# Hedgehog attention and a squared-ReLU feed-forward on one core: q loads, x buffers, the last chunk's stores, the holds of loads and the written order

## The chip, the cores and the metric

The kernel runs on one core of one Trainium2 chip. The metric is the device time of one execution in microseconds (us); lower is better. Three runs of the kernel before gave 361.65, 359.49 and 361.79 us, with a median of 361.65 us.

## What is computed

There are two stages. The first is linear attention with a feature map over q and k (8 batches, 8 heads, 576 tokens, head size 64). The second is a feed-forward over the 4608 tokens.

```python
def phi(x):
    proj = np.einsum('bhsd,df->bhsf', x, w_phi)                  # 64 -> 128
    proj = proj - np.max(np.abs(proj), axis=-1, keepdims=True)
    return np.concatenate([np.exp(proj), np.exp(-proj)], axis=-1)
q_p, k_p = (phi(q), phi(k))
kv = np.einsum('bhsf,bhsd->bhfd', k_p, v)
z = np.sum(k_p, axis=2)
num = np.einsum('bhsf,bhfd->bhsd', q_p, kv)
den = np.einsum('bhsf,bhf->bhs', q_p, z)[..., None] + 1e-06
x = (num / den), heads side by side: 4608 tokens x 512
h = np.maximum(x @ w_in, 0.0)                                    # 512 -> 2048
out = h * h @ w_out                                              # 2048 -> 512, float32
```

## The kernel before, in words

**Tiles and stages.** `attention(b)` (L295) makes x of one batch. Of the 576 tokens of a batch, 512 form a chunk of four tiles of 128 tokens; the last 64 tokens of all eight batches together form a ninth chunk. So the feed-forward has nine chunks, 0 to 8, of 512 tokens. For each chunk `ffn_in` (L710) does 16 groups of four matmuls of 128x512 (L692), a ReLU out of PSUM (L669 on ScalarE or L671 on VectorE) and a square on VectorE (L678). `ffn_out` (L751) does for each of the four token tiles 16 such matmuls in four parts (L757), a copy out of PSUM into one of three `ot` buffers (L192 or L190), and a store by SyncE's queue (L772, L775). Chunk 0 goes through `ffn_in_small` (L703), in 16 groups of sixteen 128x128 matmuls. Within attention, k and q are transposed (batches 0 and 1 by TensorE, L307; batches 2 to 7 by DMA, L317), projected with `w_phi` (L333), reduced to a maximum (L388, L489), put through two exponentials (L394, L539), and so on to `xo` (L578), which is transposed into `xT` or `xS` by a DMA of SyncE's queue (L612).

**What sets the order.** The Python builds a list of steps in program order (`Plan.add`, L61) and then issues them in the order of a list of 1755 numbers, `ORDER` (L831), which is written out by hand for all engines. Each engine takes its steps strictly in that order (`pin`, L135). `BASES` (L919) gives each step's PSUM bank, `STATES` (L926) chooses between ScalarE and VectorE for the 231 steps that may go to either, and `GATES` (L931) holds a load on the GpSimd queue until a named step has ended. `FILL` (L946) puts groups of idle matmuls (L825, 128 columns each, 120 in all) ahead of 13 TensorE steps in the first 30 us, to keep TensorE running.

**Loads.** All loads of k, q, v and weights are issued by GpSimd, with a cast from float32 to bfloat16. k and v of batches 2 to 7 come in four pieces of two heads (`load`, L240), four tokens in a row to a partition. q comes in eight (`load_q`, L259): four head pairs times two halves of two tokens each. Tile t of the q buffer (128 columns) then holds head t mod 8, tokens 2(t div 8) and the next; `q_ts` (L469) names the four tiles of a step, which lie side by side.

**Stores.** A token tile of chunks 0 to 7 is stored in one DMA of 128 rows of 2 KB (L775). A tile of the last chunk holds 64 tokens of two batches; tiles 0 to 2 are stored in two DMAs of 64 rows each (L772), on SyncE's queue. The last tile goes through `last_out` (L709) in halves of 256 columns, and each half is stored in two DMAs of 64 rows (L744), one issued by SyncE and one by ScalarE.

**Rings.** There are three `ot` buffers, three `xo` buffers (L174) and two `xT`. An `ot` copy has to wait until the store that last read its buffer has landed.

Of the kernel before, what the change touches and what calls it, by code (L numbers as in the profile page):

```python
# [15 lines left out]
SEM = 0.045  # L16
# [8 lines left out]
def dve_cost(n):  # L25
    return n / 960 + 0.064, n / 960 + 0.150 + SEM

# [80 lines left out]
def kernel(  # L108
# [52 lines left out]
    warm = sb("warm", [P])  # L161
# [9 lines left out]
    NXT = 2  # L171
    assert B * S == NCH * TCH and NCH == B + 1 and S == TCH + 64
    qp, qn = ring("qp", NQP, [8 * P]), ring("qn", NQP, [8 * P])
    xo = ring("xo", 3, [8 * D])  # L174
    rden = ring("rden", 3, [8], F32)
# [11 lines left out]
    def copy(out, in_):  # L187

        if now[0].eng == "DVE":
            pin(nc.vector.tensor_copy(out=out, in_=in_))  # L190
        else:
            pin(nc.scalar.activation(out=out, in_=in_, func=ACT.Copy))  # L192

# [65 lines left out]
    def load_q(b, jjs=(0, 1), single=True, release=False, prs=((0, 4),)):  # L259

        x = xq[b % 2]
        for jj in jjs:
# [10 lines left out]
    def of(tag, b, us):  # L273
        qs = [("xq", b % 2, u, a) for u in us if u != "s" for a in range(3)] if tag == "xq" else []
        return qs + [(tag, b % 2, u) for u in us if u != "s"] + [(tag, b % 2, "s", hi) for u in us if u == "s" for hi in range(2)]
# [19 lines left out]
    def attention(b):  # L295
# [122 lines left out]
        def scaled(t, x, n):  # L418

            e = t[:, :, D:].to_broadcast([t.shape[0], n, 2, D // 2]).rearrange("p m c x -> p m x c")  # L420
            pin(nc.vector.tensor_tensor(out=t[:, :, :D].rearrange("p m (x c) -> p m x c", c=2),  # L421
                                        in0=x.rearrange("p (m x c) -> p m x c", m=n, c=2), in1=e, op=ALU.mult))

        def v_ops(g0, g1):

            gs = [4] if g0 == 4 else list(range(g0, g1))
            for sg in range(2):
# [9 lines left out]
                def fn(t=t):  # L437
                    scaled(t[:, 8 * g0 : 8 * g1, :], xv[s2][:, 512 * g0 : 512 * g1], 8 * (g1 - g0))
                add("DVE", dve_cost(256 * (g1 - g0)), fn, r=of("xv", b, gs) + [("ve", s2, sg, g) for g in gs],
                    w=[("va", s2, sg, g) for g in gs], what="V")  # L440
# [28 lines left out]
        def q_ts(c):  # L469
            if c == 4:  # L470
                return [16, 17]
            return [8 * (c // 2) + h for h in range(8)] if first else [8 * (c // 2) + 4 * (c % 2) + i for i in range(4)]
# [36 lines left out]
        def q_ops(c):  # L509
# [3 lines left out]
            def fn():  # L513
                o = ps2(pf)
                for u in range(2):
# [5 lines left out]
                    else:  # L521
                        r = slice(64 * u, 64 * u + 64)
                        rhs = qTb[r, ts[0] : ts[-1] + 1, :]
# [19 lines left out]
        def out_ops(c):  # L543
# [27 lines left out]
            xs = xslot[0] % 3  # L571
# [92 lines left out]
    def relu_sq(g, dst, toks):  # L664
# [9 lines left out]
        def fn():  # L674
# [3 lines left out]
            pin(nc.vector.tensor_tensor(out=dst, in0=i_, in1=i_, op=ALU.mult))  # L678
        add("DVE", dve_cost(256), fn, r=[("hr", sl)], w=toks, what="sq")
# [6 lines left out]
    def ffn_in(c, mc):  # L686
# [8 lines left out]
        relu_sq(g, h2[c % 2][mc // 4][:, mc % 4, :], [("h2", c % 2, mc, tt) for tt in range(4)])  # L695

    def ffn_in_small(c, tt, mg):
# [10 lines left out]
        relu_sq(g, h2[c % 2][mg][:, :, tt * P : (tt + 1) * P], [("h2", c % 2, mg * 4 + i, tt) for i in range(4)])  # L708
# [4 lines left out]
    def last_out(c, tt, part):  # L713
# [26 lines left out]
        for half in range(2):  # L740
            for u, (name, e) in enumerate((("SP", nc.sync), ("ACT", nc.scalar))):
                def fn(half=half, u=u, e=e):
                    b = 2 * tt + u
                    pin(e.dma_start(out=out[b * S + 512 : b * S + 576, half * 256 : half * 256 + 256],  # L744
                                    in_=otl[u * 64 : u * 64 + 64, half * 256 : half * 256 + 256]))
                add(name, (0.5, 2.4), fn, r=[("otl", half)], what="stl")

    def ffn_out(c, tt, part):
# [12 lines left out]
        if part == 3:  # L761
# [6 lines left out]
            for u in range(2 if c == NCH - 1 else 1):  # L768
                def fn(u=u):
                    if c == NCH - 1:  # L770
                        b = 2 * tt + u
                        pin(nc.sync.dma_start(out=out[b * S + 512 : b * S + 576, :], in_=ot[sl][u * 64 : u * 64 + 64, :]))  # L772
                    else:
                        o = out[c * S : c * S + 512, :].rearrange("(p j) n -> j p n", j=4)[tt]
                        pin(nc.sync.dma_start(out=o, in_=ot[sl]))  # L775
                add("SP", (0.5, 0), fn, r=[("ot", sl)], dma=(0.37 if c == NCH - 1 else 0.74, HW_IN, "st"), what="st")
# [43 lines left out]
    for op in plan.arrange():  # L820
        if op.seq in FILL:
            now[0] = filler
            bank, n = FILL[op.seq]
            for _ in range(n):
                pin(nc.tensor.matmul(out=psum[:, bank, :P], lhsT=warm, rhs=warm, start=True, stop=True))  # L825
# [6 lines left out]
    4, 5, 1, 0, 9, 13, 15, 2, 3, 6, 12, 8, 14, 40, 10, 41, 11, 7, 42, 19, 43, 44, 64, 18, 46, 65, 16, 66, 45, 47,  # L832
    67, 21, 109, 68, 111, 110, 17, 70, 112, 69, 48, 144, 71, 20, 72, 119, 145, 141, 26, 120, 122, 73, 29, 146, 142,
    75, 123, 51, 22, 86, 52, 23, 50, 87, 53, 124, 76, 115, 54, 88, 116, 55, 77, 90, 89, 113, 79, 78, 56, 114, 91,
    59, 80, 27, 94, 92, 35, 83, 155, 61, 63, 95, 74, 98, 49, 34, 169, 85, 62, 104, 57, 93, 100, 25, 103, 60, 58,
    101, 158, 102, 84, 81, 99, 97, 127, 143, 105, 82, 106, 96, 159, 107, 125, 24, 128, 108, 129, 126, 156, 160, 131,
    382, 130, 170, 219, 132, 213, 157, 121, 133, 214, 147, 134, 220, 172, 148, 135, 173, 28, 117, 136, 149, 137,
    118, 174, 150, 161, 151, 199, 231, 200, 162, 183, 197, 37, 232, 184, 138, 163, 198, 33, 215, 139, 164, 187, 140,
    152, 165, 188, 380, 322, 216, 189, 36, 166, 323, 325, 153, 185, 217, 167, 154, 385, 221, 168, 233, 222, 337,
    326, 218, 331, 234, 223, 374, 334, 327, 332, 338, 224, 328, 379, 324, 225, 335, 38, 329, 175, 340, 235, 339,  # L840
    330, 376, 343, 171, 333, 236, 176, 352, 336, 341, 344, 342, 177, 190, 226, 353, 346, 178, 179, 186, 246, 381,
    261, 191, 347, 286, 180, 262, 287, 192, 355, 378, 193, 288, 194, 207, 349, 383, 208, 181, 209, 182, 264, 345,
    195, 210, 356, 502, 375, 196, 211, 265, 377, 506, 239, 350, 370, 263, 227, 245, 248, 212, 277, 367, 238, 228,
    30, 237, 240, 278, 358, 242, 229, 247, 371, 364, 244, 357, 384, 254, 253, 230, 241, 243, 510, 256, 372, 368,
    255, 39, 249, 369, 257, 373, 348, 250, 279, 251, 359, 32, 361, 351, 266, 31, 258, 354, 259, 252, 365, 280, 362,
    201, 281, 203, 260, 520, 393, 204, 202, 282, 267, 283, 295, 284, 524, 296, 268, 289, 514, 297, 290, 285, 270,
    360, 304, 271, 291, 305, 528, 392, 515, 292, 532, 366, 293, 269, 272, 306, 298, 363, 307, 299, 556, 533, 308,
    294, 205, 300, 206, 585, 560, 301, 302, 390, 309, 313, 303, 273, 310, 576, 564, 314, 274, 311, 275, 316, 276,
    315, 538, 317, 312, 575, 441, 472, 574, 442, 568, 516, 473, 577, 318, 444, 578, 319, 474, 542, 445, 571, 546,
    391, 320, 394, 573, 569, 438, 321, 395, 402, 443, 550, 589, 403, 396, 592, 503, 397, 439, 404, 582, 507, 389,  # L850
    551, 405, 499, 572, 508, 398, 446, 417, 504, 500, 454, 387, 525, 455, 509, 386, 399, 511, 526, 779, 456, 527,
    521, 388, 512, 400, 776, 410, 505, 463, 522, 517, 775, 401, 523, 580, 539, 501, 464, 593, 518, 581, 543, 440,
# [126 lines left out]
```

## Time and profile before

| what | value |
|---|---|
| runs (us) | 361.65, 359.49, 361.79; median 361.65 |
| profiled execution: span from first to last instruction | 358.8 us |
| what lies around the span, against the median | 2.85 us |
| TensorE busy | 341.0 us (95%), 3411 matmuls |
| VectorE busy | 276.7 us (77%) |
| ScalarE busy | 227.1 us (63%) |
| GpSimd busy | 112.8 us (31%), nearly all of it issuing loads |
| granted TensorE clock | 0.997 |
| DMA packets | 102631, 39.62 MB; under 512 B 77248 |
| GpSimd's queue (q0) | 51744 packets, 18.36 MB, 48.4% of 16 DMA engines |

The profile's own time is given only as a span, so the difference of 2.85 us to the median covers both what lies around a span and the difference between runs. A matmul's end is modelled in the profile: a row of four 128x512 matmuls reads 1.03 us long but the next row starts 0.87 us after it, so starts are the better measure of what a step costs TensorE. "PE" is TensorE's matmul side, "DVE" VectorE, "ACT" ScalarE, "POOL" GpSimd, "SP" SyncE; a "q" behind the name is its sequencer, which issues DMAs.

### The profile page before, as it was taken

To read this page: it belongs to the slowest core of one execution; us is meant where nothing else is said; L and a number is where in the kernel's file an instruction comes from. 1 tells how busy PE (TensorE), PEld (TensorE's weight loads), DVE (VectorE), ACT (ScalarE), POOL (GpSimd) and SP (SyncE) were. 2 spreads that over 40 slices of the span, in tenths; PEclk is the share of its full clock that TensorE was granted. 3 is DMA by queue.
4 is the path that set the end of the run, shared out by engine and by line. 5 is a ranking of instruction groups with operands and counts; after the bars stand their busy time and mean duration, and the time that the engine had idled before them with its cause. 6 is when DMAs were issued, how large, how long until landed. Compare 5 with 4: busy or idle time off the path is not lost.

```text
span 358.8 us, 8512 instructions
## 1 busy us (share of the span) xinstructions
PE 341.0 (95%) x3411; PEld 193.6 (54%) x3444; DVE 276.7 (77%) x525; ACT 227.1 (63%) x428; POOL 112.8 (31%) x167
## 2 busy tenths in 40 slices
PE   5989999979999999999999999999999998999994
PEld 4779975524554555455544644455555543444442
DVE  3999998869979997989778878799988816736210
ACT  3999887379779775796678577769777210340301
POOL 8845550784707930299301820000000000000000
PEclk9999999999999999999999999999999999999998
DMA  9999989999979998799956995600401121010105
GB/s 103 177 200 201 175 95 157 161 143 192 117 161 123 159 120 179 175 96 140 127 111 116 97 192 97 151 9 29 62 31 51 50 82 38 3 60 0 58 25 153
DMA packets 102631, 39.62 MB, mean 110 GB/s; under 512 B 77248, under 2 KB 98112, under 8 KB 102592
## 3 DMA queue, kind: packets, MB, share of 16 engines
q0 software_dynamic: 51744, 18.36, 48.4%
q1 hardware_dynamic: 50608, 20.55, 26.4%
q8 instruction: 27, 0.44, 0.5%
q10 hardware_dynamic: 240, 0.16, 0.2%
q14 instruction: 12, 0.10, 0.1%
HBM read 36.77 MB, written 9.44 MB: 129 GB/s over the span
## 4 chain that ended last, share of the span: by engine, by line
PE 72%; DVE 11%; ACT 9%; DMA 5%; issue 2%; SPq 0%; DVEq 0%; ACTq 0%; POOLq 0%
PE psum L757 27%; PE psum L692 24%; PE psum L554 5%; PE psum L333 4%; PE psum L703 3%; PE psum L449 3%; DVE va L421 3%; DMA out_dram<-ot 3%; PE psum L524 2%; ACT kp L394 2%; ACT kn L394 2%; DVE mq L489 2%; DVE h L678 2%; ACT hr L669 1%; DVE mk L367 1%
## 5 line engine op out<-in xcount | busy, mean ns | idle before, releaser
L757 PE MATMUL psum<-wout,h 128*128 128x512 bf16 x527 | 128.3, 380 | 2.5 <-issue 1.3
L692 PE MATMUL psum<-xT,win 128*128 128x512 bf16 x448 | 106.3, 379 | 3.9 <-ACT ot L192 2.5
L669 ACT ACTIVATE hr<-psum 128x512 bf16<-128x512 f32 x96 | 55.3, 596 | 48.2 <-PE psum L692 25.8
L757 PEld LDWEIGHTS <-h 128*128 128x128 bf16 x560 | 50.2, 98 | 54.3 <-issue 1.1
L692 PEld LDWEIGHTS <-win 128*128 128x128 bf16 x512 | 47.4, 97 | 58.0 <-issue 8.0
L678 DVE TENSOR_TENSOR h<-hr 128x512 bf16<-128x512 bf16 x144 | 56.4, 416 | 16.8 <-ACT hr L669 16.0
L539 ACT ACTIVATE qp<-psum 128x1024 bf16<-128x1024 f32 (+1 forms) x40 | 37.4, 940 | 23.1 <-PE psum L524 22.7
L265 POOL DMA_DIRECT2D xq<-in_q_dram x52 | 38.8, 764 | 33.8 <-ACT en L496 21.2
L489 DVE TENSOR_REDUCE mq<-psum 128x8 f32<-128x1024 f32 (+1 forms) x40 | 44.1, 1111 | 3.6 <-PE psum L333 2.9
L388 DVE TENSOR_REDUCE mk<-psum 128x8 f32<-128x1024 f32 (+1 forms) x35 | 38.2, 1111 | 3.1 <-PE psum L333 3.1
L671 DVE TENSOR_SCALAR hr<-psum 128x512 bf16<-128x512 f32 x48 | 32.8, 687 | 9.4 <-PE psum L692 7.9
L394 ACT ACTIVATE kp<-psum 128x1024 bf16<-128x1024 f32 (+1 forms) x35 | 32.8, 937 | 9.6 <-DVE mk L388 8.0
L539 ACT ACTIVATE qn<-psum 128x1024 bf16<-128x1024 f32 (+1 forms) x40 | 37.5, 940 | 1.5 <-PE psum L554 1.2
L394 ACT ACTIVATE kn<-psum 128x1024 bf16<-128x1024 f32 (+1 forms) x35 | 32.8, 937 | 0.0
L421 DVE TENSOR_TENSOR va<-xv,va 64x256 bf16<-64x256 bf16 (+2 forms) x68 | 30.4, 462 | 1.6 <-ACT va L413 0.8
L192 ACT ACTIVATE ot<-psum 128x512 f32<-128x512 f32 x18 | 10.7, 593 | 31.8 <-PE psum L757 27.3
L566 DVE TENSOR_TENSOR psum<-psum,en 128x520 f32<-128x520 f32 (+1 forms) x40 | 27.6, 698 | 3.8 <-PE psum L554 2.5
L578 DVE TENSOR_TENSOR xo<-psum,rden 128x512 bf16<-128x512 f32 (+1 forms) x40 | 27.4, 686 | 0.8
L245 POOL DMA_DIRECT2D xv<-in_v_dram x26 | 19.5, 757 | 23.3 <-DMA out_dram<-ot 20.8
L190 DVE COPY ot<-psum 128x512 f32<-128x512 f32 x17 | 11.6, 684 | 16.1 <-PE psum L757 9.4
L245 POOL DMA_DIRECT2D xk<-in_k_dram x28 | 21.1, 760 | 5.5 <-ACT va L407 3.5
L449 PE MATMUL psum<-va,kp 128*128 128x65 bf16 x256 | 19.6, 193 | 0.9 <-DVE va L421 0.4
(67 smaller groups left out, 402.4 us busy)
## 6 DMA issues: line engine op xcount, KB each, us to landing
out_dram<-ot SPq DMA_DIRECT2D x32, 256.0 KB, 2.8
xk<-in_k_dram POOLq DMA_DIRECT2D x26, 128.0 KB, 3.9
xq<-in_q_dram POOLq DMA_DIRECT2D x48, 64.0 KB, 3.9
xv<-in_v_dram POOLq DMA_DIRECT2D x24, 128.0 KB, 3.6
win<-in_moe_w_in_dram POOLq DMA_DIRECT2D x4, 512.0 KB, 11.7
wout<-in_moe_w_out_dram POOLq DMA_DIRECT2D x4, 512.0 KB, 9.4
xq<-in_q_dram POOLq DMA_DIRECT2D x4, 256.0 KB, 5.0
xv<-in_v_dram POOLq DMA_DIRECT2D x2, 512.0 KB, 9.1
```

Source lines behind the costliest of these rows:

```text
L245: pin(nc.gpsimd.dma_start(out=x[:, a * 512 : z * 512].rearrange("p (h x) -> p h x", x=4 * D), in_=src[b][2 * a : 2 * z, 0:512, :].rearrang ...
L265: pin(nc.gpsimd.dma_start(out=x[:, jj * 1024 + a * 256 : jj * 1024 + z * 256].rearrange("p (h x) -> p h x", x=128), in_=q[b][2 * a : 2 * z ...
L388: pin(nc.vector.tensor_reduce(out=mk_view(g), in_=ps2(pj)[:, :, : n * Fd].rearrange("p e (i f) -> p e i f", f=Fd), axis=AX.X, op=ALU.max, ...
L394: pin(nc.scalar.activation(out=dst[slot][:, :, :n, :].rearrange("p e i f -> p e (i f)"), in_=ps2(pj)[:, :, : n * Fd], func=ACT.Exp, scale= ...
L421: pin(nc.vector.tensor_tensor(out=t[:, :, :D].rearrange("p m (x c) -> p m x c", c=2), in0=x.rearrange("p (m x c) -> p m x c", m=n, c=2), i ...
L489: pin(nc.vector.tensor_reduce(out=mqb[:, c, :, :n], in_=ps2(pj)[:, :, : n * Fd].rearrange("p e (i f) -> p e i f", f=Fd), axis=AX.X, op=ALU ...
L539: pin(nc.scalar.activation(out=o, in_=i_, func=ACT.Exp, scale=sgn))
L669: pin(nc.scalar.activation(out=hr[sl], in_=ps1(g), func=ACT.Relu))
L671: pin(nc.vector.tensor_scalar(out=hr[sl], in0=ps1(g), scalar1=0.0, scalar2=None, op0=ALU.max))
L678: pin(nc.vector.tensor_tensor(out=dst, in0=i_, in1=i_, op=ALU.mult))
L692: pin(nc.tensor.matmul(out=o, lhsT=win[mc // 4][:, kc, mc % 4 * P : (mc % 4 + 1) * P], rhs=x, start=(kc == 0), stop=(kc == KC - 1)))
L757: pin(nc.tensor.matmul(out=ps1(g), lhsT=h2[c % 2][mc // 4][:, mc % 4, tt * P : (tt + 1) * P], rhs=wout[mc // 4][:, mc % 4, :], start=(mc = ...
```

## The change

1. **q of batches 2 to 7** is loaded by four tokens of a head pair, as k and v are: four DMAs of 128 KB to a batch in place of eight of 64 KB. The tiles of a step then lie two apart, so the moving operand of the projection (L524) steps over every second tile.
2. **Five `xo` and `rden` buffers** in place of three.
3. **The last chunk's tiles** are stored whole: one DMA of 128 rows for tiles 0 to 2, and one DMA of 128 rows for each half of the last tile. The pattern on the output side is two blocks of 64 rows, 576 rows apart.
4. **GATES** names 108 loads in place of 131, other steps for each; **ORDER**, **BASES** and **STATES** are new. By the flags, three ReLUs, five `ot` copies and three transposed copies move from VectorE to ScalarE and two `kv` copies the other way.
5. **FILL** has 90 matmuls of 248 columns ahead of 14 steps, and writes them in part into columns from 264 on of a bank in use; `warm` is 256 columns wide.
6. `pool_cost`, `engine()` and `plan.either((o, "POOL", ...))` could move work to GpSimd, but `LENT = 0` turns all of it off.

```diff
-    xo = ring("xo", 3, [8 * D])
-    rden = ring("rden", 3, [8], F32)
+    xo = ring("xo", 5, [8 * D])
+    rden = ring("rden", 5, [8], F32)
...
         x = xq[b % 2]
+        if b >= 2:
+            for a, z in prs:
+                def fn(a=a, z=z):
+                    pin(nc.gpsimd.dma_start(
+                        out=x[:, a * 512 : z * 512].rearrange("p (h x) -> p h x", x=4 * D),
+                        in_=q[b][2 * a : 2 * z, 0:512, :].rearrange("h (p j) d -> p h (j d)", j=4)))
...
+            jjs = ()
         for jj in jjs:
...
-            return [8 * (c // 2) + h for h in range(8)] if first else [8 * (c // 2) + 4 * (c % 2) + i for i in range(4)]
+            if first:
+                return [8 * (c // 2) + h for h in range(8)]
+            return [(8 * (c // 2) + 4 * (c % 2) + i) if pe_in else 8 * (c % 2) + 2 * i + c // 2 for i in range(4)]
...
-                        rhs = qTb[r, ts[0] : ts[-1] + 1, :]
+                        rhs = qTb[r, ts[0] : ts[-1] + 1 : ts[1] - ts[0], :]
...
-        for half in range(2):
-            for u, (name, e) in enumerate((("SP", nc.sync), ("ACT", nc.scalar))):
-                def fn(half=half, u=u, e=e):
-                    b = 2 * tt + u
-                    pin(e.dma_start(out=out[b * S + 512 : b * S + 576, half * 256 : half * 256 + 256],
-                                    in_=otl[u * 64 : u * 64 + 64, half * 256 : half * 256 + 256]))
-                add(name, (0.5, 2.4), fn, r=[("otl", half)], what="stl")
+        for half, (name, e) in enumerate((("ACT", nc.scalar), ("SP", nc.sync))):
+            def fn(half=half, e=e):
+                o = out.rearrange("(b s) n -> b s n", s=S)[2 * tt : 2 * tt + 2, 512:576, half * 256 : half * 256 + 256]
+                pin(e.dma_start(out=o, in_=otl[:, half * 256 : half * 256 + 256]))
+            add(name, (0.5, 2.6), fn, r=[("otl", half)], what="stl")
...
-            for u in range(2 if c == NCH - 1 else 1):
-                def fn(u=u):
-                    if c == NCH - 1:
-                        b = 2 * tt + u
-                        pin(nc.sync.dma_start(out=out[b * S + 512 : b * S + 576, :], in_=ot[sl][u * 64 : u * 64 + 64, :]))
...
+            def fn():
+                if c == NCH - 1:
+                    o = out.rearrange("(b s) n -> b s n", s=S)[2 * tt : 2 * tt + 2, 512:576, :]
+                    pin(nc.sync.dma_start(out=o, in_=ot[sl]))
...
-            bank, n = FILL[op.seq]
+            bank, n, col = FILL[op.seq]
             for _ in range(n):
-                pin(nc.tensor.matmul(out=psum[:, bank, :P], lhsT=warm, rhs=warm, start=True, stop=True))
+                pin(nc.tensor.matmul(out=psum[:, bank, col : col + 248], lhsT=warm[:, :P], rhs=warm[:, :248], start=col == 0, stop=True,
+                                     skip_group_check=True))
...
 ORDER = [
-    4, 5, 1, 0, 9, 13, 15, 2, 3, 6, 12, 8, 14, 40, 10, 41, 11, 7, 42, 19, 43, 44, 64, 18, 46, 65, 16, 66, 45, 47,
...
+    4, 3, 8, 7, 13, 0, 5, 15, 6, 9, 1, 12, 10, 64, 19, 65, 11, 2, 66, 18, 68, 67, 111, 109, 21, 112, 110, 40, 69,
```

What the new order says, read out step by step for the places that the prediction uses:

- On SyncE's queue the first stores stand as follows. Before: q transpose of batch 2, an x transpose of batch 1, k transpose of batch 2, three x transposes, the first store. After: q transpose, k transpose, the first store, then the x transposes.
- Ahead of the first matmul group of the feed-forward (L703), the new order has eight matmuls of a k projection and four transposes of x (L594) on TensorE that the old one had behind it. On VectorE only the new order has there: a maximum of 128x1024 (L388), three copies of 128x256 into `xT` (L603), one copy of 128x512 and one of 128x256 of transposed k or q, and two `kv` copies of 128x260 (all L190). Only the old one had: one copy into `xT`, one of 128x512 and one of 128x256 of transposed k or q, and one `kv` copy.
- TensorE changes between steps of 64 rows (the projections, L333, L482, L360 and L524) and steps of 128 rows 114 times in the old order and 124 times in the new one.
- The new order ends on TensorE with three parts of the last chunk's tile 1, all four parts of chunk 7's tile 1, the last part of the last chunk's tile 1, and then the four parts of its tile 2 as the last matmuls of all. SyncE's last entries are the stores of chunk 7's tile 1 and of the last chunk's tiles 1, 0 and 2; both halves of the last tile are stored earlier. In the old order the last matmuls were the first half of the last tile, 256 columns wide, and SyncE's last entries were the six half stores of tiles 0 to 2 and one of the last tile.

## The prediction on record

> **What bounds the kernel now.** I read the page first: the engines' busy shares, then the slices. TensorE is busy in all but the first and last slices, so time can be won only at the two ends and in the few places where TensorE stands still.
>
> ```profile
> span 358.8 us, 8512 instructions
> ...
> PE 341.0 (95%) x3411; PEld 193.6 (54%) x3444; DVE 276.7 (77%) x525; ACT 227.1 (63%) x428; POOL 112.8 (31%) x167
> ...
> PE   5989999979999999999999999999999998999994
> ```
>
> The reader is to see 95% for TensorE, a 5 at the start and an 8 in the third slice, a 7 in the ninth, an 8 in the thirty-fourth and a 4 at the end. Next I read the waits, those of TensorE and those of the engines that held it up:
>
> ```profile
> ACT ot L192 <- DMA out_dram<-ot: 4.5, 1, 4.5
> ...
> PE psum L692 <- ACT ot L192: 2.5, 1, 2.5
> ...
> PE psum L692 <- DVE ot L190: 1.2, 1, 1.2
> ```
>
> So TensorE's two long waits in the steady part (2.5 us in the ninth slice, 1.2 us in the thirty-fourth) are waits for a copy into an `ot` buffer, and the copy waited for an old store to land. SyncE's own timeline shows why that store was late:
>
> ```profile
> 51.73 6.95 SPq L317 DMA_TRANSPOSE qT<-xq  x1
> 58.73 1.25 SPq L612 DMA_TRANSPOSE xT<-xo  x1
> 60.15 3.73 SPq L317 DMA_TRANSPOSE kT<-xk  x1
> 63.93 3.90 SPq L612 DMA_TRANSPOSE xT<-xo  x3
> 67.94 0.52 SPq L775 DMA_DIRECT2D out_dram<-ot  x1
> ```
>
> The first store stood behind six transposes. Last I read the end of the timeline and the stores by windows of time:
>
> ```profile
> 352.82 1.47 PE L721 MATMUL psum<-wout,h 128*128 128x256 bf16 x12
> ...
> 354.33 0.38 ACT L737 ACTIVATE otl<-psum 128x256 f32<-128x256 f32 x1 [0.71 <-PE psum L721]
> ...
> 355.41 0.74 SPq L744 DMA_DIRECT2D out_dram<-otl  x1
> ```
>
> ```profile
> 318.80:321.80 3.00, 2.95 (x15) 1.34 (x14) 2.02 (x5) 1.89 (x4) 0.00 (x0) 1.00 0.45 175
> ...
> 352.30:356.00 3.70, 2.00 (x16) 1.27 (x13) 0.00 (x0) 0.98 (x2) 0.00 (x0) 1.00 0.76 178
> ```
>
> TensorE ends at 352.82 + 1.47 = 354.3 and the span at 358.8: the drain is 4.5 us. The last two columns of the windows are the mean busy share of the 16 DMA engines and GB/s. In the first window two whole tiles of 128 rows are stored: 175 / (16 x 0.45) = 24.3 GB/s per busy engine. In the second, halves of 64 rows: 178 / (16 x 0.76) = 14.6. Rows of the same 2 KB go at different rates, so a store's time hangs on how its rows are spread, not on its bytes.
>
> **The change part by part.**
>
> *q loads.* 48 DMAs of 64 KB become 24 of 128 KB: 24 issues fewer at 764 ns (group L265) are 18.3 us of GpSimd, which is busy 31%. Issue to landing is 3.9 us for both sizes in the page's issue rows. Nothing of TensorE's waits after 30 us names a load, so this counts as nothing; the work that hides it is the matmul stream. The moving operand that steps over every second tile costs nothing either: L692 already reads `xT` that way at 379 ns, beside 380 ns of L757, which reads in a row.
>
> *Five x buffers.* No wait in the profile is for an x buffer: 0.
>
> *Work moved to ScalarE.* VectorE loses about three ReLUs (687 ns), five `ot` copies (684) and a net 0.4 us of small copies: 5.9 us; ScalarE gains about as much. At 77% and 63% both have room: 0.
>
> *The first store.* It moves ahead of four x transposes (1.25 + 3.90 us, all now behind it), so it is issued about 4 us earlier, near 64 us. With the 6.3 us that it took to land it is there near 70.2, and the copy, ready at 69.7, hardly waits. The 2.5 us go. Late next are the four x transposes, which chunk 1 needs: 64.5 + 5.2 + 2.5 us landing = 72.2, about when TensorE gets there. The 1.2 us at 298 go as well: there two stores of chunk 6 were issued together from 293.78 on, the second of them behind the first on SyncE's queue though its copy was long done; in the new order each follows its copy. Sum: -3.7 us. The bounds are 0 (another copy is late) and -3.7.
>
> *Changes of row mode.* Four matmuls of L692 that start at 124.44 are followed by a 64-row step at 125.39 (0.95 us); four at 125.72 by a 128-row step at 126.59 (0.87). So a change costs about 0.1 us, and ten more cost +1.0 us.
>
> *The first phase.* Ahead of the first feed-forward group VectorE has a maximum (1.22 us), two net copies into `xT` (0.28 each) and one net `kv` copy (0.42) more: +2.2 us. VectorE is busy 23.86 of the first 30 us. If it is the path all the way, the start slips by 2.2; if it starts to work earlier than at 9 us, by nothing. TensorE has 0.5 us more of its work behind it by then. I take +1.0, between 0 and +2.2. The idle matmuls go from 120 x 54 ns to about 90 x 104 (by columns), +2.9 us on TensorE, which has 5.5 us free in these 30 us: 0, at worst +2.9.
>
> *Holds.* 108 loads wait for other steps, and the new ones lie nearer to their use: some v pieces are released only 5.5 us of TensorE steps ahead of the scaling that reads them, and issue plus landing are 0.76 + 3.9 = 4.7 us. I take +0.5, between 0 and +3.
>
> *The last chunk's stores.* This is the term that decides, and no row shows it. Each store is now one DMA whose output pattern is two blocks of 64 rows. From below: it goes like any whole tile, 2.8 us (issue rows, 256 KB). From above: the two blocks are the unit that is spread, so two engines move it. Then 262144 B / 2 / 24.3 GB/s = 5.4 us of movement in place of 262144 / 16 / 24.3 = 0.7, and at 14.6 GB/s 9.0. The rows are nearest to 24.3, since the rows are the same 2 KB from 128 partitions. Every transfer in the trace has 64 or 128 equal steps outermost on both sides, so none can say which; the two windows above, where the number of rows in a step alone changed the rate, make me take the spread by blocks.
>
> The Trainium skill, "DMA: Bandwidth & Descriptors", section on why a DMA increments its semaphore by 16, says that the number of engines is the largest up to 16 that divides the slowest dimension of both patterns. By that it is 2 here; no run here shows it. The same page's "Rules for kernel authors" says that two transfers of disjoint partition halves are better made as one: by that alone the whole tile is the better store.
>
> The last three stores then run one behind the other on the same two engines. Tile 1's copy ends about 3.46 us (four parts of 0.865) less 0.2 + 0.7 before TensorE's end, so its store is issued 2.5 us before the end; a store's time besides movement is 2.8 - 0.7 = 2.1. End: -2.5 + 2.1 + 3 x 5.4 = 15.8 us behind TensorE's last matmul, in place of 4.5: **+11.3 us**. With whole-tile pricing it is a 0.6 us copy, 0.1 and 2.8 us: 3.5 to 4.1, so -0.6.
>
> *Sum:* -3.7 + 1.0 + 1.0 + 0.5 = -1.2, and +11.3: +10.1. The profiled span of 358.8 becomes 368.9; what lies around it (2.85 to the median; the lowest run lies 0.7 above the span) is taken as unchanged. 361.65 + 10.1 = **371.7 us**.
>
> **The rivals.**
>
> *Whole-tile pricing.* If two blocks are spread over all engines, the sum is -1.2 - 0.6 = -1.8, and the time 359.9 us; with first phase and holds at nothing, 358.3, and with an earlier start of VectorE 357. For it speaks that stores of 128 rows go at the better rate in the windows. It decides on a single point: whether a last-chunk store lands in about 2.8 us or in over 7.
>
> *Loads come late.* The stores are cheap, but the holds are too tight: TensorE gets waits behind VectorE's scaling. At 1 us in each of six batches, the time is 359.9 + 6 = 366. Against it: 4.7 us against 5.5, so most would fit. It decides once landings go from 3.9 to over 4.7 us, as the store at 67.94 did with 6.3.
>
> *The change of order does nothing at 72 us.* Then the 2.5 us stay, and each time above rises by as much; this widens the ranges and is no case of its own.
>
> **How the numbers follow.** About 1% (3.6 us) is what a measurement of this kernel can tell from no change. Two-engine stores 0.68 (slower); whole-tile pricing 0.22, of which 0.08 faster by over 1% and 0.14 within; late loads 0.10 (slower). So faster 0.08, same 0.14, slower 0.78. The likeliest case's own range is 366 (first phase, holds at nothing, stores overlapping their fixed parts) to 377 (the -3.7 not won, holds +2). From below I add whole-tile pricing down to 358; above 377 lie the stores at 14.6 GB/s (3 x 3.6 us more), which I leave out.
>
> **What would show it.** Two-engine stores: last-chunk stores landing in 7 to 18 us, and 15 us with no engine busy behind TensorE's last matmul. The first store: issued near 64 us, no TensorE wait behind `ot` in the ninth slice. First phase: the first L703 at 30 to 32 us (30.0 now). q: 12288 packets of 256 B (48 x 256) become 6144 of 512 B, so "under 512 B" falls from 77248 to about 64960. I am wrong if the drain stays near 4.5 us, or if TensorE shows new waits behind V (L421).

## The result and the profile after

The changed kernel takes 374.63 us (three runs, 374.46 to 374.69) against 361.65 us before: a ratio of 1.036, 95% interval 1.031 to 1.041. That is 13.0 us slower; 10.1 us were forecast, and 371.7 us. The two profiled spans lie further apart, 358.8 and 372.9 us: 14.1 us. In each run of this case that gives both, the time is 1.7 to 2.2 us above the span, so the execution of the kernel before that the profile shows would have taken about 360.6 us (an estimate from these differences), less than the median of 361.65.

The page of the changed kernel, from the same places that were read before (span, busy time, slices of TensorE, granted clock):

```profile
span 372.9 us, 8499 instructions
...
PE 346.6 (93%) x3382; PEld 196.1 (53%) x3414; DVE 272.4 (73%) x516; ACT 235.1 (63%) x437; POOL 95.6 (26%) x143
...
PE   7798999899999999999999999999999999999920
...
PEclk9989999999999999999999999999999999999985
```

The 7 in the ninth slice and the 8 in the thirty-fourth are gone; one 8 stands in the eighth. But the last two slices, 9.3 us each, read 2 and 0, slices two to four read 7, 9, 8 where they read 9, 8, 9, and the clock is down in the third. So the time went to the two ends. The waits of the changed kernel, the old `ot` wait and the longest one of TensorE:

```profile
ACT ot L197 <- DMA out_dram<-ot: 8.2, 2, 5.7
...
PE psum L849 <- DVE warm L234: 1.1, 1, 1.1
```

ScalarE still waits for stores, but no wait of TensorE names `ot` any more, and the longest that is left is the one for the operand of the idle matmuls at the very start. SyncE's timeline shows why (start, length, line, transfer, how many):

```profile
61.74 0.37 SPq L799 DMA_DIRECT2D out_dram<-ot  x1
65.84 10.24 SPq L637 DMA_TRANSPOSE xT<-xo  x4
76.20 3.08 SPq L799 DMA_DIRECT2D out_dram<-ot  x2
```

The first store goes out at 61.7 us, ahead of the x transposes, 6.2 us earlier than the 67.94 of before. The end of the timeline:

```profile
345.87 10.52 PE L782 MATMUL psum<-wout,h 128*128 128x512 bf16 x47
...
353.70 4.79 SPq L796 DMA_DIRECT2D out_dram<-ot  x3
...
356.43 0.60 ACT L197 ACTIVATE ot<-psum 128x512 f32<-128x512 f32 x1 [0.65 <-PE psum L782]
```

TensorE ends at 345.87 + 10.52 = 356.4 us and the span at 372.9: a drain of 16.5 us in place of 4.5. What runs in it, by windows (busy time of each engine, then granted clock, mean share of the 16 DMA engines, GB/s):

```profile
359.00:362.00 3.00, 0.00 (x0) 0.00 (x0) 0.00 (x0) 0.00 (x0) 0.00 (x0) 0.76 0.13 51
...
368.00:371.00 3.00, 0.00 (x0) 0.00 (x0) 0.00 (x0) 0.00 (x0) 0.00 (x0) 0.50 0.13 51
```

No engine works, and the DMA share is 0.13, which is 2/16: two DMA engines move 51 GB/s, 25.5 each, for some 12 us on end. The packet records of the trace agree: from 358 to 371 us two packets of 2 KB are under way at a time, each 84 ns long. The three stores of 262144 B last 5.1 us each at that rate.

The other end is the first phase. The first feed-forward matmul of chunk 0 starts at 29.85 us before and at 35.54 us after:

```profile
29.85 1.06 PE L703 MATMUL psum<-xT,win 128*128 128x128 bf16 x16
```

```profile
35.54 2.63 PE L730 MATMUL psum<-xT,win 128*128 128x128 bf16 x44
```

The stretch from 20 to 30 us of the kernel before, and then of the changed one (columns: TensorE, its weight loads, VectorE, ScalarE, GpSimd, clock, DMA share, GB/s; the DMA share adds up the times of all packets under way and so can exceed 1):

```profile
20.00:30.00 10.00, 9.17 (x185) 7.57 (x185) 9.89 (x24) 9.42 (x23) 5.07 (x7) 1.00 1.34 200
```

```profile
20.00:30.00 10.00, 9.78 (x158) 8.03 (x157) 7.92 (x17) 8.34 (x21) 2.77 (x5) 0.87 1.39 200
```

VectorE worked 9.9 of the 10 us before and 7.9 after, and TensorE was granted 0.87 of its clock. The phase isn't longer because more work lies in it; the engines wait more. VectorE's timeline shows for what. Before, the scalings of v (`va`) run in one row:

```profile
18.48 3.75 DVE L421 TENSOR_TENSOR va<-xv,va 128x512 bf16<-128x512 bf16 x11
```

After, the last five stand behind two maxima, and the first of these waits for TensorE:

```profile
23.48 1.23 DVE L514 TENSOR_REDUCE mq<-psum 128x8 f32<-128x1024 f32 x1 [2.04 <-PE psum L507]
24.63 0.68 DVE L388 TENSOR_REDUCE mk<-psum 128x4 f32<-128x512 f32 x1
25.23 1.76 DVE L442 TENSOR_TENSOR va<-xv,va 128x512 bf16<-128x512 bf16 x5
```

The first k'v matmul, which needs the scaled v, starts at 25.00 us in place of 20.67, 4.3 us late; the first matmul that uses k'v is 5.0 us late (29.26 and 24.25), and the feed-forward 5.7. What VectorE waited for at 23.48 is the q projection, which is queued behind 16 idle matmuls; those took 3.37 us, 0.21 us each:

```profile
19.53 3.37 PE L849 MATMUL psum<-warm 128*128 128x248 bf16 x16
22.83 0.62 PE L507 MATMUL psum<-wphi,qT 64*128 64x128 bf16 x8
```

The windows of the changed kernel around them:

```profile
17.00:18.00 1.00, 0.42 (x3) 0.25 (x3) 1.00 (x4) 1.00 (x2) 0.70 (x1) 1.00 1.48 193
...
20.00:21.00 1.00, 1.00 (x7) 0.70 (x6) 1.00 (x3) 0.91 (x3) 0.14 (x2) 0.50 1.58 196
...
22.00:23.00 1.00, 1.00 (x8) 0.60 (x7) 0.00 (x0) 1.00 (x5) 0.61 (x1) 0.68 1.27 205
```

TensorE is busy 0.42 to 0.64 of each microsecond from 15 to 19 us, and then gets half its clock from 19.2 to 22.6 us (by the clock of the windows from 19 to 23).

So the account of the two spans, 372.9 - 358.8 = 14.1 us: drain +12.0, start of the feed-forward +5.7, the two `ot` waits -2.5 and -1.2, all else +0.1. The last term is what is left over; none of its parts is measured by it.

### The profile page after: what moved, and what is told of

Read it like the earlier page. It is cut to its first block, busy times and chain, and to the rows that moved or that the text cites. A ratio compares the mean times of both kernels' runs of the same rounds, so it can differ in the third digit from the quotient of the medians.

```text
span 372.9 us, 8499 instructions
## 1 busy us (share of the span) xinstructions
PE 346.6 (93%) x3382; PEld 196.1 (53%) x3414; DVE 272.4 (73%) x516; ACT 235.1 (63%) x437; POOL 95.6 (26%) x143
## 2 busy tenths in 40 slices
DMA packets 95952, 39.60 MB, mean 106 GB/s; under 512 B 64426, under 2 KB 91434, under 8 KB 95914
## 4 chain that ended last, share of the span: by engine, by line
PE 75%; DVE 5%; ACT 2%; issue 2%; DMA 2%; POOL 1%; POOLq 0%; DVEq 0%
PE psum L782 30%; PE psum L719 26%; PE psum L579 5%; PE psum L354 4%; PE psum L472 3%; PE psum L730 3%; PE psum L549 2%; DMA xv<-in_v_dram 2%; DVE mq L514 1%; DVE psum L591 1%; PE psum L748 1%; DVE va L442 1%; PE psum L477 1%; DVE mk L409 1%; POOL xq L273 1%
## 5 line engine op out<-in xcount | busy, mean ns | idle before, releaser
L719 PE MATMUL psum<-xT,win 128*128 128x512 bf16 x448 | 105.1, 379 | 0.0
L694 ACT ACTIVATE hr<-psum 128x512 bf16<-128x512 f32 x99 | 58.2, 599 | 46.4 <-PE psum L719 37.2
L703 DVE TENSOR_TENSOR h<-hr 128x512 bf16<-128x512 bf16 x144 | 57.3, 418 | 12.6 <-ACT hr L694 11.5
L564 ACT ACTIVATE qp<-psum 128x1024 bf16<-128x1024 f32 (+1 forms) x40 | 37.1, 937 | 15.4 <-PE psum L549 15.1
L696 DVE TENSOR_SCALAR hr<-psum 128x512 bf16<-128x512 f32 x45 | 30.8, 686 | 7.8 <-PE psum L719 6.9
L197 ACT ACTIVATE ot<-psum 128x512 f32<-128x512 f32 x23 | 13.7, 596 | 34.9 <-PE psum L782 26.4
L603 DVE TENSOR_TENSOR xo<-psum,rden 128x512 bf16<-128x512 f32 (+1 forms) x40 | 27.1, 683 | 0.8
L195 DVE COPY ot<-psum 128x512 f32<-128x512 f32 x12 | 8.3, 688 | 21.5 <-PE psum L782 18.5
L273 POOL DMA_DIRECT2D xq<-in_q_dram x24 | 17.0, 708 | 16.5 <-PE psum L579 4.3
```

The lines of the kernel that those rows point to most:

```text
L564: pin(nc.scalar.activation(out=o, in_=i_, func=ACT.Exp, scale=sgn))
L694: pin(nc.scalar.activation(out=hr[sl], in_=ps1(g), func=ACT.Relu))
L703: pin(engine().tensor_tensor(out=dst, in0=i_, in1=i_, op=ALU.mult))
L719: pin(nc.tensor.matmul(out=o, lhsT=win[mc // 4][:, kc, mc % 4 * P : (mc % 4 + 1) * P], rhs=x, start=(kc == 0), stop=(kc == KC - 1)))
```

## The experiments

The theory after the result: the last chunk's stores run on two DMA engines each and cost 12 us; the new order of the first phase costs 5 to 6 us; the stores moved ahead win about 4 us; all else is small. The rivals are told with each run. Times are medians beside runs of the kernel before on the same chip (360.7, 361.2 and 361.6 us in the three groups, each on a chip of its own); ratios are to those.

**Stores of the changed kernel in halves.** Only the last chunk's stores go back to 64 rows each:

```diff
-                    o = out.rearrange("(b s) n -> b s n", s=S)[2 * tt : 2 * tt + 2, 512:576, :]
-                    pin(nc.sync.dma_start(out=o, in_=ot[sl]))
+                    for u in range(2):
+                        b = 2 * tt + u
+                        pin(nc.sync.dma_start(out=out[b * S + 512 : b * S + 576, :], in_=ot[sl][u * 64 : u * 64 + 64, :]))
```

(the same for the `otl` halves). 

> The changed kernel with the last chunk's tiles stored in halves of 64 rows again, from the same steps and in the same order. Theory (the two-block stores run on two DMA engines, and this alone makes the drain 16.5 us): the drain falls to about 4.5 us and the time by 12, from 374.6 to 362.6 us. Rival (the drain is long because the order now ends with a full tile and three stores in a row, however they are spread): the time stays above 370.

Measured: 365.1 us, ratio 1.013 (1.006 to 1.019). Its drain in the windows:

```profile
358.00:363.00 5.00, 0.43 (x2) 0.00 (x0) 0.00 (x0) 0.60 (x1) 0.00 (x0) 0.80 0.47 110
```

The same bytes in twice as many DMAs move at 110 GB/s instead of 51, and the drain is 4.8 us, 11.7 less, as the theory had it. But the time falls by 9.5 us and not by 12. In the execution shown, TensorE ends 2.0 us later than in that of the changed kernel (358.4 and 356.4 us): 0.3 us of it are there at the first feed-forward matmul, and most of the rest comes at 97.5 us, where TensorE waits for a scaled v:

```profile
PE psum L472 <- DVE va L442: 1.0, 1, 1.0
```

The profile of the changed kernel has no such wait. What is left against the kernel before is 4.4 us; the runs on the first phase below ask where it lies.

**The kernel before with whole-tile stores in the last chunk.** The converse of the last edit, and nothing else. 

> The kernel before with this one part of the change: the last chunk's tiles and the two halves of its last tile are stored whole, in the old order. Theory: on two engines the three tiles need 64 x 84 ns = 5.4 us each and the two halves about 3 each, one behind the other from 349.9 on, so the span ends near 349.9 + 22.1 + 0.5 = 372.5 and the time goes from 361.65 to about 375. Rival (whole-tile pricing, and fewer issues on SyncE): 361 or a little less.

Measured: 378.02 us, ratio 1.049 (1.042 to 1.056). Two windows of it, one at 75 us and one in the drain:

```profile
75.00:78.00 3.00, 1.80 (x5) 0.68 (x5) 0.05 (x1) 2.42 (x5) 1.98 (x3) 0.50 1.73 138
...
364.00:368.00 4.00, 0.00 (x0) 0.00 (x0) 0.00 (x0) 0.00 (x0) 0.00 (x0) 0.50 0.13 50
```

In the drain again two engines move 25 GB/s each. It takes 19.9 us here, longer than after the change, mostly because the last half of `otl` (131072 B, 2.6 us at 50 GB/s), which ScalarE issues at 358.3 us, has to share the two engines with the other three stores. The first window belongs to another matter: in this execution TensorE's wait for `ot` at 72 us was 3.3 us, and half the clock followed until about 82 us. TensorE ends 3.5 us later than before (357.8 and 354.3 us), and the time is 3 us above the theory's 375. Of the 17.3 us, 15.4 are the longer drain (19.9 and 4.5 us).

**The kernel before with q loaded by four tokens.** Only `load_q`, its tokens and the step of L524 are those of the change:

```diff
+        if b >= 2:
+            for a, z in prs:
...
+                        in_=q[b][2 * a : 2 * z, 0:512, :].rearrange("h (p j) d -> p h (j d)", j=4)))
-                        rhs = qTb[r, ts[0] : ts[-1] + 1, :]
+                        rhs = qTb[r, ts[0] : ts[-1] + 1 : ts[1] - ts[0], :]
```

> The kernel before with only the q loads of batches 2 to 7 by four tokens (24 DMAs of 128 KB in place of 48 of 64 KB, and the projection stepping over every second tile), in the old order; the holds of the second half's DMA fall away. Theory (hidden by the matmul stream): 361.65 within 1 us. Rival (the loads and their packets slow the stores and transposes that share the engines): 2 to 3 us faster.

Measured: 360.72 us, ratio 1.001 (0.997 to 1.004). GpSimd is busy 95.9 us instead of 112.8, and the time doesn't move.

**The kernel before with two stores moved ahead.** In `ORDER` the first store (516) goes ahead of the x transpose 294, and the store of chunk 6's fourth tile (1647) right behind that of its third.

```diff
-    294, 205, 300, 206, 585, 560, 301, 302, 390, 309, 313, 303, 273, 310, 576, 564, 314, 274, 311, 275, 316, 276,
+    516, 294, 205, 300, 206, 585, 560, 301, 302, 390, 309, 313, 303, 273, 310, 576, 564, 314, 274, 311, 275, 316,
```

 

> The kernel before with two entries of the order moved: the first store of chunk 0 ahead of three x transposes on SyncE's queue, and the store of chunk 6's tile 3 ahead of that of tile 1. Theory: TensorE's waits of 2.5 us at 72 and 1.2 us at 298 go, and the time falls by 3.7 to about 358. Rival (the next thing is late, the x transposes or a copy, and takes the time back): 361 to 362.

Measured: 358.19 us, ratio 0.992 (0.989 to 0.995). TensorE's waits:

```profile
PE psum L692 <- DVE ot L190: 1.6, 1, 1.6
...
PE psum L333 <- DVE xo L578: 0.9, 1, 0.9
```

The 2.5 us at 72 us are gone. The wait at 298 us stays (1.6 us in place of 1.2), since I had moved the wrong store for it, and a small one for an x buffer comes. The fall of the median by 2.5 us is not the wait alone, since in some executions of the kernel before a stretch of half clock goes with it (last section): against the twelve runs of this group whose mean clock was 0.997 or more, with a median of 359.6 us, it is 1.4 us.

**The changed kernel (stores in halves) with the old order at its head,** in two lengths. First up to 24 us, the first 136 steps:

```diff
 ORDER = [
-    4, 3, 8, 7, 13, 0, 5, 15, 6, 9, 1, 12, 10, 64, 19, 65, 11, 2, 66, 18, 68, 67, 111, 109, 21, 112, 110, 40, 69,
+    4, 5, 1, 0, 9, 13, 15, 2, 3, 6, 12, 8, 14, 40, 10, 41, 11, 7, 42, 19, 43, 44, 64, 18, 46, 65, 16, 66, 45, 47,
...
```

> The changed kernel with its last-chunk stores in halves, and with the first 136 steps of the old order put back at its head (steps up to about 24 us, with the old filler matmuls and engine choices there). Theory, that the first phase costs 5.6 us by its new order and that about half of it is lost by 24 us, at the stretch of half clock: first L730 near 32 to 33 us instead of 35.9 and about 362.5 us instead of 365.1. Rival, that the loss lies behind 24 us: first L730 still at 35 to 36 us and 365 us. Second rival, that a joint between two orders makes a wait of its own: above 365 us.

Measured: 364.54 us, ratio 1.008 (1.004 to 1.012), first L730 at 35.06 us. The v scalings run early again and the k'v matmuls start at 20.74 us, as before; but then TensorE waits:

```profile
PE psum L855 <- DVE kT L195: 1.5, 1, 1.5
PE psum L328 <- DVE qT L195: 1.1, 1, 1.1
```

The copies it waits for are of batch 1, and the new order has them ahead of batch 0's steps: the first matmul that uses k'v (L579) comes at 28.78 us, 24.25 before. So the first rival holds: the old order up to 24 us alone wins nothing that stands out of the spread (0.6 us by the medians; the ten runs go from 362.9 to 367.3 us, and the profile is of the fastest). The joint may add to that; it can't be told apart here.

Then with the first 352 steps of the old order, past the first feed-forward groups. 

> As the run before, but with the first 352 steps of the old order (up to about 62 us of compute; the DMA transposes and stores of the queue of SyncE stay where the changed kernel has them). Theory, that the whole rest of the slowdown (365.1 against 360.7 us) is the first phase: first L730 near 30 to 31 us and 360 us, within 1 us. Rival, that the lost time comes back later whatever the start is, because loads or stages behind it set the pace: 363 to 365 us.

Measured: 360.23 us, ratio 0.999 (0.996 to 1.002). The first feed-forward matmul on TensorE's timeline:

```profile
30.33 1.06 PE L730 MATMUL psum<-xT,win 128*128 128x128 bf16 x16
```

It starts 5.5 us earlier than at 35.88 in the run with half stores, and 4.9 us of the time go with it. So the steps up to 352 hold the rest of the slowdown. But this run has the changed kernel's first store ahead and is still no faster than the kernel before. It has two waits of its own, up to 60.8 and up to 76.9 us:

```profile
PE psum L328 <- DVE ot L195: 1.4, 1, 1.4
...
PE psum L719 <- DMA xT<-xo: 1.0, 1, 1.0
```

Whether they come from the joint of the two orders, and so hide what the moved stores win, stays open.

**A bridge of idle matmuls.** The changed kernel with half stores and 18 more idle matmuls at the two longest waits of 15 to 18 us:

```diff
-    135: (2, 3, 264),
+    135: (2, 3, 264), 158: (2, 8, 264), 117: (2, 10, 264),
```

> The changed kernel with its last-chunk stores in halves, and with 18 more filler matmuls, 8 ahead of the third feature matmul and 10 ahead of the transposes of q's short block, where TensorE had waited 0.9 and 1.1 us at 15.4 to 18.0 us. Theory, that these waits lead to the half clock of 19.6 to 23.0 us and that the half clock delays the work behind it: clock 1.00 there, first L730 about 1.7 us earlier (near 34.2 us), 363.3 us. Rival, that VectorE and ScalarE pace this phase and TensorE's clock there costs nothing: first L730 still at 35.9 us and 365 us.

Measured: 363.59 us, ratio 1.008 (1.004 to 1.011), first L730 at 34.53 us. Two of its windows:

```profile
17.00:18.00 1.00, 0.74 (x8) 0.68 (x8) 0.90 (x3) 0.98 (x3) 0.43 (x1) 1.00 1.50 194
...
20.00:21.00 1.00, 1.00 (x14) 0.91 (x11) 0.87 (x2) 0.74 (x2) 0.97 (x3) 1.00 1.37 204
```

The clock stays at 1.00 from 20 to 23 us. The 16 idle matmuls ahead of the q projection, 3.43 us in the run with half stores, now take 1.87:

```profile
20.03 1.87 PE L852 MATMUL psum<-warm 128*128 128x248 bf16 x16
```

The feed-forward starts 1.35 us earlier. So about 1.4 us of the late start were the half clock, and by subtraction the rest is the order itself. That the time falls with it is less sure. The medians differ by 1.5 us, but they are those of 4 runs (363.9 to 366.4 us) and 10 runs (362.7 to 366.9) on two chips, and the two profiled executions took 365.0 and 364.9 us: in the one with the bridge TensorE waits 1.0 us for v at 97 us, and half its clock is gone from 98.2 to 101.6 us.

**Four output buffers.** The kernel with two stores ahead, and besides:

```diff
-    ot = ring("ot", 3, [DM], F32)
+    ot = ring("ot", 4, [DM], F32)
...
-            sl = oslot[0] % 3
+            sl = oslot[0] % 4
```

With four, the third store of chunk 2 comes behind the next copy into its buffer, so one tile of 36 holds another's values; the run is read for its waits and its time, and is no kernel to keep. 

> The kernel before with the two stores moved ahead (358.2 us by itself) and four output buffers instead of three. Theory, that the wait of TensorE at 298 us comes from the copy that has to wait for the store of the tile three back: that wait of 1.6 us goes too, and the time is 356.6 us, 356 to 357.5. Rival, that what follows the wait has its own limit (loads of the next batch, or the row of copies on ScalarE), so that the 1.6 us come back as another wait: 358 us.

Measured: 357.72 us, ratio 0.991 (0.988 to 0.995). The wait at 298 us goes, but one like it stands at 142 us:

```profile
PE psum L333 <- DVE ot L190: 1.6, 1, 1.6
```

There a store had been issued only at 140.2 us, again the second of two behind one another:

```profile
139.76 0.81 SPq L775 DMA_DIRECT2D out_dram<-ot  x2
```

So both were partly right: the buffers move the wait, and the time is the rival's. What the two places share is the late issue on SyncE's queue; the next run tests it.

**Three stores ahead.** That queueing, in the kernel before, at 294 us: SyncE issues two stores one behind the other,

```profile
293.78 0.81 SPq L775 DMA_DIRECT2D out_dram<-ot  x2
```

the first for chunk 6, whose copy has just ended, the second (1575) the last of chunk 5, whose copy ended at 268.6 us. The edit takes 1575 from its place behind 1593 (the store of chunk 6) and puts it right behind 1557, besides the two moves above; three buffers stay:

```diff
-    1473, 1480, 1474, 1579, 1546, 1475, 1563, 1540, 1481, 1476, 1572, 1489, 1524, 1482, 1558, 1490, 1557, 1541,
...
-    1496, 1497, 1498, 1623, 1597, 1591, 1601, 1592, 1627, 1593, 1575, 1588, 1605, 1589, 1602, 1645, 1628, 1499,
...
+    1540, 1481, 1476, 1572, 1489, 1524, 1482, 1558, 1490, 1557, 1575, 1541, 1491, 1633, 1492, 1493, 1583, 1542,
...
+    1601, 1592, 1627, 1593, 1588, 1605, 1589, 1602, 1645, 1628, 1499, 1580, 1646, 1500, 1584, 1501, 1581, 1594,
```

> The kernel before with three stores moved ahead: the two of the earlier run (358.2 us), and the fourth store of chunk 5, whose copy is done at 267 us but which SyncE issues only at 293 us, behind the first store of chunk 6, which waits for its own copy. Theory, that the remaining wait of TensorE at 297 us (1.6 to 1.7 us) comes from this queueing alone: it goes, 356.6 us (356 to 357.3). Rival, that the buffer comes free early but another limit takes over at 298 us (rows of copies on VectorE, the next transposes): 358 us.

Measured: 356.68 us, ratio 0.990 (0.984 to 0.996). SyncE's timeline now:

```profile
280.44 1.05 SPq L775 DMA_DIRECT2D out_dram<-ot  x2
...
290.69 0.33 SPq L775 DMA_DIRECT2D out_dram<-ot  x1
```

The store of chunk 5 is the second of the two at 280 us now, instead of 294, and no wait of TensorE names `ot`. So the late issue was the cause of the wait at 298 us. The median is 1.5 us below that with two stores ahead, as the theory had it, and the runs don't overlap (356.2 to 357.0 and 357.7 to 359.9 us); but the two groups ran on two chips, and by the ratios the gain is 0.9 us, within their intervals. This beats both kernels.

**Five x buffers on top of that.**

```diff
-    xo = ring("xo", 3, [8 * D])
+    xo = ring("xo", 5, [8 * D])
```

(`rden` and the slot counter likewise). 

> The run before this with five x buffers instead of three. In the profile with the stores ahead, the DMA transposes queue behind the first store, VectorE waits 1.2 us at 71 us for an x buffer and TensorE 0.9 to 1.1 us for VectorE. Theory, that the five buffers are worth nothing alone but take away just this wait: 355.6 us, 1.0 us under the run with three buffers. Rival, that the wait of TensorE there is covered or comes back within some microseconds: the same time as with three buffers, within 0.4 us.

Measured: 356.45 us, ratio 0.987 (0.984 to 0.991): the same time. The run says less than it was meant to, since the profile with three stores ahead doesn't show the x wait that the one with two had. Five buffers are worth nothing measurable; whether they cover that wait when it comes stays open.

**No holds.** The changed kernel with half stores, `GATES = {}`. 

> The changed kernel with its last-chunk stores in halves (365.1 us) and without any of its holds for loads: a load is issued as soon as its place in the queue of GpSimd and its free buffer allow. Theory, that the holds cost the 1.2 us wait for a late v at 97.5 us and little else: that wait goes, 364.0 us (363.3 to 365). Rival, that the holds keep loads from colliding with the transposes and the stores, so that more is lost than won: above 365.5 us, with longer waits for transposes (xT, kT, qT). Second rival, that the holds do nothing, since buffers and queue order set the loads: 365.1 us.

Measured: 368.32 us, ratio 1.022 (1.014 to 1.030), 3.2 us slower than with the holds (four runs each, on two chips: 366.0 to 370.2 and 363.9 to 366.4 us). The wait for v at 97.5 us is gone, and this one comes at 79 us:

```profile
PE psum L719 <- DMA xT<-xo: 3.6, 1, 3.6
```

The window in which those x transposes are under way, without holds:

```profile
70.00:74.00 4.00, 3.91 (x48) 2.09 (x47) 3.71 (x7) 0.69 (x2) 4.00 (x7) 1.00 1.70 141
```

The same window of the run with half stores and all holds:

```profile
70.00:74.00 4.00, 3.90 (x49) 2.11 (x47) 3.70 (x8) 0.61 (x2) 1.33 (x2) 1.00 0.34 43
```

Without holds GpSimd issues loads all the time there (4.00 of 4 us against 1.33), and the DMA share is 1.70 against 0.34. The four x transposes are issued at the same time in both runs, from 66 us on, but take longer to land without holds; first with them, then without:

```profile
DMA to landing us min/median/max: 2.3/3.1/3.7
```

```profile
DMA to landing us min/median/max: 6.3/6.7/7.6
```

The first rival holds: the holds keep the loads away from the transposes. Part of the 3.2 us is clock again, which is at half from 83.7 to 87.1 us, behind the wait. The run says what all holds are worth, not what the change from the old ones to the new ones did.

## Why the prediction was right or wrong

It was right in sign and in the term that decides, and the time came out 2.9 us above it, inside its range. By the spans it was 4.0 us short (10.1 and 14.1 us): the first phase was 4.7 us too small and the last stores 0.7, and 1.4 us that it had put on holds and row modes, and that the account above doesn't find, made up for part of it. That the time was met to 3 us is partly luck: these errors went against each other, and what lies around the span, taken as the same 2.85 us, was 1.7 us after. By its steps:

| step | forecast, us | measured, us |
|---|---|---|
| last chunk's stores | +11.3 | +12.0 (drain); 9.5 when undone |
| `ot` waits | -3.7 | both gone (-2.5 and -1.2); -2.5 and about -1.5 by the medians with stores ahead |
| first phase | +1.0, bounds 0 and +2.2 | +5.7; 4.9 of the time when undone; about 1.4 of the start is the clock |
| holds | +0.5 | no wait for v in the changed kernel's profile, 1.0 us in two runs with half stores; 3.2 worse without any |
| row modes | +1.0 | not measured alone |
| q loads, x buffers, work to ScalarE | 0 | 0, 0, not measured alone |

*The last chunk's stores.* The step held: the spread goes by the two blocks of the output pattern. The rate of 24.3 GB/s to an engine, taken from the window with whole tiles, was 25.5, and the drain 16.5 us where 15.8 was said, 15.9 of them without any engine's work. The Trainium skill, "DMA: Bandwidth & Descriptors", section on why a DMA increments its semaphore by 16, gives two engines by its rule of the largest divisor, and the windows at 0.13 agree. The advice in the same page's "Rules for kernel authors", one transfer in place of two of disjoint partition halves, would have made the whole tile the better store; both runs speak against it for this pattern (+17.3 us on the kernel before, 15.4 of them in the drain; 9.5 us won back on the changed one). The rival of whole-tile pricing fell.

*The first store, and the wait at 298 us.* The first wait goes in a run that changes only the order of stores. That its median fell by just the 2.5 us of the wait is in part chance, since some of it is clock. For the second wait the reading was nearly right: a store whose copy was long done stood behind another. It was the last of chunk 5 and not one of chunk 6, and so the first experiment moved the wrong one.

*The first phase* is the step that failed. It counted the work that the new order puts ahead of the first feed-forward group on VectorE (2.2 us), and took that sum as the upper bound. Such a sum bounds the delay only while VectorE never waits. The trace shows it waiting: 7.9 us busy of 10 in place of 9.9. The new order puts maxima of later steps ahead of the scalings of v, and copies of batch 1 ahead of batch 0's steps; each engine takes its steps strictly in order, so one late operand (the q projection behind 16 idle matmuls) holds up all that stands behind it. The idle matmuls were costed at 104 ns each, with 2.9 us at worst; at half clock they took 0.21 us. Nothing in the forecast asked whether TensorE would be idle long enough at 15 to 19 us to lose its clock.

*Holds.* The wait behind v that was feared isn't in the profile of the changed kernel. It shows in two of the runs with half stores, once in each, 1.0 us near 97.5 us; the rival of late loads at 1 us in each of six batches fell. That holds win something was not in the forecast at all: it had only asked what they delay.

*q loads.* 0, with the run to show it, though a q load of 128 KB took 6.0 us to land in the changed kernel, and 4.9 in that run, and not 3.9. Packets under 512 B fell to 64426 (about 64960 was said).

*Row modes.* Left open. All terms but the drain, the start and the `ot` waits sum to +0.1 us in the account above, so ten changes at 0.1 us are at most hidden in it.

## What to carry to other kernels

Write a store so that the outermost dimension on both sides has many equal steps; two blocks outermost left 14 of 16 DMA engines idle here, and at the end nothing covers it. On a queue that is taken strictly in order, look for each wait at when the issue went out and what stood ahead of it: moving three stores in the list won 1.0% here, where a fourth buffer only moved the wait. Where an order is changed, don't bound the delay by the sum of work put ahead; follow the one chain (here scaled v, k'v, the first x) and ask of each step whether its operand is there, and look for gaps of TensorE in which it may lose its clock.

## What the runs showed of the hardware that I had not expected

In the changed kernel TensorE lost half its clock without ever standing still for long: it was busy 0.42 to 0.64 of each microsecond from 15 to 19 us, with no wait over 0.9 us, while in the run with the bridge it was busy 0.62 and more and kept it. The Trainium skill, "TensorE: Matmul & The Clock Gate", Part 1, tells of a monitor that halves the clock after an idle window of about 3.4 us, and under "A second HAM failure mode" of a kernel in which frequent short idle times do it; the first phase here is like the second. But the runs give no threshold: in the kernel before, TensorE was busy 0.42, 0.00 and 0.12 of the microseconds from 72 to 75 us and kept its clock.

A wait of TensorE's of the same length may or may not do it. In the kernel before, the one of 2.5 us at 72 us left the clock at 1.00 in the profile shown. In the run with q by four tokens, which has the same order, it was just as long, and half the clock followed:

```profile
PE psum L700 <- ACT ot L192: 2.5, 1, 2.5
...
76.00:79.00 3.00, 3.00 (x8) 0.91 (x6) 0.69 (x1) 2.39 (x5) 3.00 (x6) 0.50 1.44 192
```

In the run with whole stores the wait was 3.3 us, and the clock was at 0.50 from 75 us on. Each such stretch lasted 3.4 us, in the run with whole stores 6.8. That goes with the spread of the kernel before, 358.3 to 364.8 us in the 59 runs beside the experiments: the 26 with a mean clock of 0.995 or less took 360.9 us and more, the 33 others, all at 0.997 or more, 362.2 and less. With three stores ahead no such wait is left; the 14 runs took 356.1 to 357.7 us, none with a mean clock under 0.998.
